# Turning keys, queries and normalised tokens in the DMA crossbar instead of on TensorE

## The chip, the cores and the metric

The kernel runs on one core of one Trainium2 chip. The metric is the device time of one execution in microseconds (us), the median of several runs. Engines: PE is TensorE's matmuls, PEld its weight loads, DVE is VectorE, ACT is ScalarE, POOL is GpSimd, SP is the sync engine. DMAs are issued from POOL (loads that cast from 32 to 16 bits) and from SP (stores, copies inside SBUF, the core's working memory, and the crossbar DMAs). The profile counts both kinds on the core's 16 DMA engines. L288 and the like are line numbers of the kernel; they differ from version to version.

## The reference, cut to what matters

Four batches of 768 tokens, 8 heads of 64. Attention goes by chunks of 32 queries, each with 8 memory keys and up to 56 keys around it. The result is the x of a feed-forward block: normalise x, multiply by a 512x2048 matrix, clip at zero, multiply by a 2048x512 matrix, add x.

```python
for c in range(nc):                       # chunks of 32 tokens
    k_full = concat([mem_k, k[:, :, l_start:r_end]])
    v_full = concat([mem_v, v[:, :, l_start:r_end]])
    scores = scale * q_c @ k_full.T
    out[c] = softmax(scores) @ v_full
x  = out.reshape(B, S, 512)
xn = (x - mean) / sqrt(var + 1e-6) * g_ln
out = x + maximum(xn @ w_ch1, 0) @ w_ch2
```

## The kernel before: the parts that the change touches

The matmuls here contract over partitions, so three things must be turned to have their features on partitions: keys (KT), queries (QZ) and the normalised tokens (xT). Before, all three were turned on TensorE by a matmul with the identity, and the result was copied out of PSUM, the memory into which the matmuls write.

```python
def turn_kq(pv, src, j, n):               # 128 of these matmuls a batch
    for r in range(8):
        for par in range(2):
            nc.tensor.matmul(
                out=pv[64 * par : 64 * par + 64, n * r : n * r + n],
                lhsT=src[0:n, 2 * j + par, r, :], rhs=identity[0:n, 0:n],
                is_transpose=True, start=True, stop=True,
                tile_position=(0, 64 * par))

def load_kq(b, which, lo=0, hi=96, h0=0, h1=H):   # runs of 512 values, 2 KB
    ...
        in_=dram(src, (b * H + h0) * HS + 512 * lo,
                 [[512, hi - lo], [HS, h1 - h0], [1, 512]]))

def turn_x(u, i, t, kind="att"):          # 4 matmuls a tile of 128 tokens
    for dt in range(4):
        nc.tensor.matmul(out=pv[:, 128 * dt : 128 * dt + 128],
            lhsT=xn[t % 3][:, 128 * dt : 128 * dt + 128], rhs=identity,
            is_transpose=True, start=True, stop=True)
    nc.scalar.copy(out=xT[u % 2][:, :, 128 * i : 128 * i + 128], in_=...)
```

The work is laid out by hand: eight units of three tiles of 128 tokens. A unit has 28 steps, 16 "up" steps (first matrix) and 12 "down" steps (second matrix). The attention of the following unit, the turns and the loads are hung on these steps. Units 2 and 4 prepare batches 2 and 3.

```python
elif u in (2, 4):
    attend(((1, 8, 8, 12), (4, 8, 10, 14), (11, 17, 17, 21)))   # scores, values, norm, turn_x
    b = u // 2 + 1
    for j, step in ((0, 17), (2, 23)):
        at(step, kq_block, b, j, 0, NG, "mm")
        at(step, keep_rest)
    for h in range(H):
        at(2 + 2 * h, load_v_head, b, h)
    ...
elif following:
    attend(((12, 17, 17, 21), (14, 17, 17, 22), (18, 23, 23, 26)))
```

The softmax here doesn't subtract the row's maximum and nothing guards it: scores larger than these inputs give would overflow.

## Time and profile before

| | before |
|---|---|
| median time | 231.82 us (231.43 to 232.01, three runs); 231.62 with a fourth |
| span of the profiled run | 230.2 us |
| PE busy | 222.8 us, 97% |
| idle time of PE, by its list of waits | 3.7 us, all before 49 us |
| DVE, ACT, POOL busy | 54%, 52%, 30% |

Busy time is what the profile counts for an engine; the list of waits names, for each idle stretch, who ended it.

### The profile page before, as it was taken

The page shows a single profiled execution, that of the slowest core. Times are in us where ns is not written, and L with a number is a line of the kernel's source. Part 1 is how long each engine was busy: PE and PEld are TensorE (multiplying, and loading weights), DVE is VectorE, ACT ScalarE, POOL GpSimd, SP SyncE. Part 2 cuts the span into 40 slices and gives each one's busy share as a digit, 9 for nine tenths or more (in the row PEclk, how much of TensorE's full clock was granted, in tenths as well). Part 3 has the DMA queues.
Part 4 walks back from the last instruction along what each step waited for, and adds up shares of the span by engine and source line. Part 5 has one row for each costly group of instructions (what it writes and reads, how often), then busy time and mean ns, then how long its engine had stood idle before and what let it go on. Part 6 is the DMA issues. An engine that isn't in the chain of part 4 may idle for free.

```text
span 230.2 us, 5499 instructions
## 1 busy us (share of the span) xinstructions
PE 222.8 (97%) x2289; PEld 138.2 (60%) x2289; DVE 125.4 (54%) x290; ACT 119.0 (52%) x228; POOL 68.6 (30%) x125
## 2 busy tenths in 40 slices
PE   7989999899999999999999999999999999999993
PEld 2455776447765577555765577556765566557553
DVE  5746881475747639575336648674436542663222
ACT  3565648253894576655355367654356335534200
POOL 6973343877360380530001370410001200030000
PEclk9999999999999999999999999999999999999999
DMA  5999999999999999548921199543001200111012
GB/s 80 169 90 203 201 211 150 125 200 226 121 69 126 226 145 36 37 77 119 236 48 48 48 127 23 37 99 106 0 3 46 90 4 0 47 48 46 0 48 93
DMA packets 50307, 21.91 MB, mean 95 GB/s; under 512 B 37817, under 2 KB 46777, under 8 KB 50234
## 3 DMA queue, kind: packets, MB, share of 16 engines
q0 software_dynamic: 45680, 14.23, 90.1%
q1 hardware_dynamic: 4602, 7.33, 10.5%
q8 instruction: 18, 0.29, 0.6%
q14 instruction: 7, 0.06, 0.1%
HBM read 28.48 MB, written 6.29 MB: 151 GB/s over the span
## 4 chain that ended last, share of the span: by engine, by line
PE 77%; DMA 16%; POOL 2%; DVE 2%; issue 1%; POOLq 0%
PE mm L319 32%; PE mm L336 32%; DMA w2c<-in_moe_w_ch_dram 13%; PE att L238 4%; DMA V<-in_v_dram 3%; PE att L258 3%; PE att L176 3%; PE att L296 2%; POOL V L114 2%; PE mm L354 2%; PE mm L176 1%; DVE QZ L374 1%; DVE V L379 0%; DVE V L378 0%; DVE osb L359 0%
## 5 line engine op out<-in xcount | busy, mean ns | idle before, releaser
L319 PE MATMUL mm<-xT,w1c 128*128 128x384 f16 x512 | 88.3, 326 | 0.0
L336 PE MATMUL mm<-w2c,rT 128*128 128x512 f16 x368 | 87.4, 379 | 0.2 <-DMA w2c<-in_moe_w_ch_dram 0.2
L319 PEld LDWEIGHTS <-w1c 128*128 128x128 f16 x512 | 57.0, 114 | 24.2 <-issue 0.3
L327 DVE TENSOR_SCALAR rT<-mm 128x384 f16<-128x384 f32 x64 | 35.5, 556 | 35.3 <-PE mm L319 35.1
L336 PEld LDWEIGHTS <-rT 128*128 128x128 f16 x368 | 33.8, 98 | 34.0 <-issue 0.3
L325 ACT ACTIVATE rT<-mm 128x384 f16<-128x384 f32 x64 | 31.2, 489 | 35.9 <-PE mm L319 33.9
L245 ACT ACTIVATE AT<-att,band 96x512 f16<-96x512 f32 x48 | 30.1, 677 | 17.1 <-PE att L238 16.6
L287 POOL TENSOR_SCALAR veps<-squares 128x1 f32<-128x1 f32 x24 | 4.5, 188 | 109.9 <-ACT junk L284 95.1
L343 DVE SCALAR_TENSOR_TENSOR osb<-mm,rstd,xs 128x512 f32<-128x512 f32 x23 | 17.2, 749 | 30.9 <-PE mm L336 20.4
L114 POOL DMA_DIRECT2D V<-in_v_dram x24 | 21.5, 900 | 15.5 <-DMA V<-in_v_dram 4.5
L301 ACT COPY xT<-att 128x512 f16<-128x512 f16 x21 | 12.2, 581 | 23.8 <-PE att L296 23.8
L191 DVE COPY KT<-att 128x80 f16<-128x80 f16 (+3 forms) x44 | 18.4, 480 | 2.1 <-PE att L176 2.1
L278 DVE SCALAR_TENSOR_TENSOR xn<-xs,nmean,g_row 128x512 f16<-128x512 f32 x24 | 18.0, 752 | 0.9
L201 ACT COPY QZ<-mm 64x768 f16<-64x768 f16 (+1 forms) x18 | 13.6, 757 | 8.0 <-PE mm L176 7.8
L268 DVE RECIPROCAL rec<-att 128x8 f32<-128x8 f32 x24 | 4.9, 203 | 23.3 <-PE att L258 23.3
L284 ACT ACTIVATE junk<-xs,nmean 128x512 f16<-128x512 f32 x24 | 17.4, 724 | 0.1
L269 DVE SCALAR_TENSOR_TENSOR xs<-att,rec 128x512 f32<-128x512 f32 x24 | 16.6, 691 | 0.8
L238 PE MATMUL att<-QZ,KT 128*128 128x128 f16 x192 | 14.8, 219 | 0.9 <-ACT AT L245 0.6
L238 PEld LDWEIGHTS <-KT 128*128 128x128 f16 x192 | 12.6, 98 | 4.6 <-issue 1.4
L201 ACT COPY QZ<-att 64x384 f16<-64x384 f16 (+1 forms) x20 | 12.0, 598 | 5.3 <-PE att L176 5.1
L291 POOL TENSOR_TENSOR rstd<-veps,mhalf 128x1 f32<-128x1 f32 x24 | 13.3, 553 | 2.0
L258 PEld LDWEIGHTS <-AT 96*64 96x64 f16 x384 | 7.9, 111 | 8.7 <-issue 6.0
(63 smaller groups left out, 145.5 us busy)
## 6 DMA issues: line engine op xcount, KB each, us to landing
out_dram<-osb SPq DMA_DIRECT2D x23, 256.0 KB, 5.9
w1c<-in_moe_w_ch_dram POOLq DMA_DIRECT2D x4, 512.0 KB, 12.0
w2c<-in_moe_w_ch_dram POOLq DMA_DIRECT2D x4, 512.0 KB, 15.7
V<-in_v_dram POOLq DMA_DIRECT2D x20, 88.0 KB, 14.1
k<-in_k_dram POOLq DMA_DIRECT2D x2, 768.0 KB, 12.4
q<-in_q_dram POOLq DMA_DIRECT2D x2, 768.0 KB, 16.1
V<-in_v_dram POOLq DMA_DIRECT2D x16, 96.0 KB, 5.9
k<-in_k_dram POOLq DMA_DIRECT2D x3, 256.0 KB, 6.3
```

The costliest lines, as they stand in the source:

```text
L114: nc.gpsimd.dma_start(out=V[b % 2][r : r + hi - lo, g, :, 0:64], in_=dram(v, b * H * HS + lo * D, [[64, hi - lo], [HS, H], [1, 64]]),)
L191: copy(out=free(KT[b % 2], j * KC + 24 + 32 * ga + 8 * lo, [[KR, gb - ga], [8, m], [1, 8]]), in_=free(pv, lo, [[8, gb - ga], [1, m], [n, 8]]),
L201: copy(out=free(QZ[b % 2][rows, j, g0, par, :], 0, [[128, g1 - g0], [8, 8], [1, 8]]), in_=free(pv[rows, :], 8 * g0, [[8, g1 - g0], [1, 8], ...
L238: nc.tensor.matmul(out=p[:, gg, 128 * j : 128 * j + 128], lhsT=KT[b % 2][:, j, KR * g : KR * g + 128], rhs=QZ[b % 2][:, j, g, :, :], start ...
L245: nc.scalar.activation(out=free(a, 32 * c, [[512, 2], [64, 8], [1, 32]], KR), in_=free(p, 32 * c, [[512, 2], [64, 8], [1, 32]], KR), func= ...
L278: nc.vector.scalar_tensor_tensor(out=xn[i], in0=x, scalar=nmean[i], in1=g_row, op0=ALU.add, op1=ALU.mult,)
L284: nc.scalar.activation(out=junk, in_=xs[xi], func=ACTF.Square, bias=nmean[i], accum_out=squares[i],)
L319: nc.tensor.matmul(out=p, lhsT=free(w, i, [[4, 128]]), rhs=xT[u % 2][:, dt, 0 : 128 * n], start=(dt == 0), stop=(dt == 3),)
L325: nc.scalar.activation(out=o, in_=p, func=ACTF.Relu)
L327: nc.vector.tensor_scalar(out=o, in0=p, scalar1=0.0, scalar2=None, op0=ALU.max)
L336: nc.tensor.matmul(out=p, lhsT=rT[hc][:, 128 * i : 128 * i + 128], rhs=w2c[hc // 4][:, hc % 4, :], start=(hc == 0), stop=(hc == 15),)
L343: nc.vector.scalar_tensor_tensor(out=o, in0=p, scalar=rstd[t % 9], in1=xs[t % 9], op0=ALU.mult, op1=ALU.add,)
```

## The change

Its intent: take the turns off the bound engine. Keys and queries of batches 2 and 3 are loaded with one token per partition (runs of 64 values, 256 B) and turned by crossbar DMAs ("crossings" below), four a batch. The queries carry columns of zeros, so that the crossing writes the block layout that the scores want. x is turned by crossbar for two of the three tiles of unit 2 and for all later units. The key columns are laid out anew (memory keys last), and the schedule is moved. The core of the diff:

```diff
+    def load_k_tokens(b, t):
+        nc.gpsimd.dma_start(out=free(kraw[0], 512 * t, [[64, H], [1, 64]]),
+            in_=dram(k, b * H * HS + 128 * t * D, [[D, 128], [HS, H], [1, 64]]))
+    def cross_k(b, half):
+        nc.sync.dma_start_transpose(
+            out=free(KT[b % 2], half * 24 * KR + 16, [[KR, 24], [1, 64]]),
+            in_=kraw[0][64 * half : 64 * half + 64, 0:3072])
+    def cross_q(b, half):
+        nc.sync.dma_start_transpose(
+            out=free(QZ[b % 2], half * 24 * 128, [[64, 48], [1, 64]]), in_=qraw[0][rows, :])
     def turn_x(u, i, t, kind="att"):
+        if kind == "dma":
+            nc.sync.dma_start_transpose(
+                out=xT[u % 2][:, :, 128 * i : 128 * i + 128], in_=xn[t % 3])
+            return
 ... (unit 1)
-            for which in range(2):
-                at(1, load_kq, 2, which)
-            attend(late)
+            at(1, clear_raw)
+            for t in range(6):
+                at(23, load_tokens, 2, t)
+            attend(((16, 19, 19, 19), (17, 19, 20, 20), (21, 23, 23, 26)), "att")
 ... (units 2 to 6)
-            attend(((12, 17, 17, 21), (14, 17, 17, 22), (18, 23, 23, 26)))
+            attend(((9, 14, 14, 14), (11, 14, 15, 15), (16, 20, 20, 20)))
+            if u in (2, 4):
+                for half in range(2):
+                    at(21, cross_k, b, half)
+                for half in range(2):
+                    at(22, cross_q, b, half)
+                at(24, mem_cols, b); at(24, k_around, b)
+                at(25, v_mem, b);    at(25, v_around, b)
             if u == 3:
-                for which in range(2):
-                    at(2 + which, load_kq, 3, which)
+                for t in range(6):
+                    at(21, load_tokens, 3, t)
 ... (value rows and masks moved by 8 rows, place(), k_around(): cut)
```

More of the change, by code (lines that the diff above doesn't have):

```diff
@@ L34 @@
     KR = 96
-    KC = NG * KR + 32
     HD = 65
@@ L58 @@
     w2c = [sb.tile([128, 4, 512], FP16, name=f"w2c{i}") for i in range(4)]
-    k16 = [sb.tile([96, H, 8, 64], FP16, name=f"k16_{i}") for i in range(2)]
-    q16 = [sb.tile([96, H, 8, 64], FP16, name=f"q16_{i}") for i in range(2)]
+    kraw = [sb.tile([128, 4096], FP16, name=f"kraw{i}") for i in range(2)]
+    qraw = [sb.tile([128, 4096 if i else 6144], FP16, name=f"qraw{i}") for i in range(2)]
+    k16 = [t[0:96, 0:4096].rearrange("p (h r d) -> p h r d", h=H, r=8) for t in kraw]
+    q16 = [t[0:96, 0:4096].rearrange("p (h r d) -> p h r d", h=H, r=8) for t in qraw]
     V = [sb.tile([128, NG, H, HD], FP16, name=f"V{i}") for i in range(2)]
-    KT = [sb.tile([128, 4, KC], FP16, name=f"KT{i}") for i in range(2)]
-    QZ = [sb.tile([128, 4, NG, 2, 64], FP16, name=f"QZ{i}") for i in range(2)]
+    KT = [sb.tile([128, NG * 4 * KR + 32], FP16, name=f"KT{i}") for i in range(2)]
+    QZ = [sb.tile([128, NG, 4, 2, 64], FP16, name=f"QZ{i}") for i in range(2)]
     AT = [sb.tile([128, 2, H, 64], FP16, name=f"AT{i}") for i in range(3)]
@@ L112, in load_v_group @@
         lo, hi = max(64 * g - 16, 0), min(64 * g + 72, S)
-        r = 24 + lo - 64 * g
+        r = 16 + lo - 64 * g
         nc.gpsimd.dma_start(
@@ L120, in load_v_head @@
         nc.gpsimd.dma_start(
-            out=V[b % 2][24:88, :, h, 0:64],
+            out=V[b % 2][16:80, :, h, 0:64],
             in_=dram(v, (b * H + h) * HS, [[64, 64], [64 * 64, NG], [1, 64]]),
@@ L127, in v_around @@
         vt = V[b % 2]
-        nc.sync.dma_start(out=vt[8:24, 1:NG, :, :], in_=vt[72:88, 0 : NG - 1, :, :])
-        nc.sync.dma_start(out=vt[88:96, 0 : NG - 1, :, :], in_=vt[24:32, 1:NG, :, :])
+        nc.sync.dma_start(out=vt[0:16, 1:NG, :, :], in_=vt[64:80, 0 : NG - 1, :, :])
+        nc.sync.dma_start(out=vt[80:88, 0 : NG - 1, :, :], in_=vt[16:24, 1:NG, :, :])
     def v_mem(b):
@@ L133, in v_mem @@
         nc.sync.dma_start(
-            out=V[b % 2][0:8, :, :, :],
+            out=V[b % 2][88:96, :, :, :],
             in_=bass.AP(tensor=src.tensor, offset=src.offset,
@@ L166, in mem_cols @@
         nc.vector.tensor_copy(
-            out=free(KT[b % 2], 0, [[KC, 4], [KR, NG], [1, 8]]),
+            out=free(KT[b % 2], KR - 8, [[KR, 4], [4 * KR, NG], [1, 8]]),
             in_=bass.AP(tensor=src.tensor, offset=src.offset,
@@ L191, in keep_k @@
                 copy(
-                    out=free(KT[b % 2], j * KC + 24 + 32 * ga + 8 * lo,
-                             [[KR, gb - ga], [8, m], [1, 8]]),
+                    out=free(KT[b % 2], (4 * ga + j) * KR + 16 + 8 * (lo - 8 * ga),
+                             [[4 * KR, gb - ga], [8, m], [1, 8]]),
                     in_=free(pv, lo, [[8, gb - ga], [1, m], [n, 8]]),
@@ L201, in keep_q @@
         copy(
-            out=free(QZ[b % 2][rows, j, g0, par, :], 0, [[128, g1 - g0], [8, 8], [1, 8]]),
+            out=free(QZ[b % 2][rows, g0, j, par, :], 0, [[512, g1 - g0], [8, 8], [1, 8]]),
             in_=free(pv[rows, :], 8 * g0, [[8, g1 - g0], [1, 8], [n, 8]]),
@@ L230, in keep_rest, with place, clear_raw, load_q_tokens @@
         kept_later.pop(0)()
+    def place(b, g):
+        return g if b < 2 else g % 2 * (NG // 2) + g // 2
+    def clear_raw():
+        nc.gpsimd.memset(free(qraw[0], 64, [[256, 24], [1, 128]]), 0.0)
+    def load_k_tokens(b, t):
+        nc.gpsimd.dma_start(
+            out=free(kraw[0], 512 * t, [[64, H], [1, 64]]),
+            in_=dram(k, b * H * HS + 128 * t * D, [[D, 128], [HS, H], [1, 64]]),
+        )
+    def load_q_tokens(b, t, par):
+        nc.gpsimd.dma_start(
+            out=free(qraw[0], 1024 * t + 192 * par, [[256, H // 2], [1, 64]]),
+            in_=dram(q, (b * H + par) * HS + 128 * t * D, [[D, 128], [2 * HS, H // 2], [1, 64]]),
+        )
+    def load_tokens(b, t):
+        load_k_tokens(b, t)
+        for par in range(2):
+            load_q_tokens(b, t, par)
+    def cross_k(b, half):
+        nc.sync.dma_start_transpose(
+            out=free(KT[b % 2], half * 24 * KR + 16, [[KR, 24], [1, 64]]),
+            in_=kraw[0][64 * half : 64 * half + 64, 0:3072],
+        )
+    def cross_q(b, half):
+        rows = slice(64 * half, 64 * half + 64)
+        nc.sync.dma_start_transpose(
+            out=free(QZ[b % 2], half * 24 * 128, [[64, 48], [1, 64]]), in_=qraw[0][rows, :]
+        )
+    def k_around(b):
+        n, odd, kt = 24, 24 * KR, KT[b % 2]
+        for dst, src, m, w in (
+            (odd, 64, n, 16), (4 * KR, odd + 64, n - 4, 16),
+            (80, odd + 16, n, 8), (odd + 80, 4 * KR + 16, n - 4, 8),
+        ):
+            nc.gpsimd.tensor_copy(
+                out=free(kt, dst, [[KR, m], [1, w]]), in_=free(kt, src, [[KR, m], [1, w]])
+            )
     def scores(b, t):
@@ L235, in scores @@
         for gg in range(2):
-            g = 2 * t + gg
+            g = place(b, 2 * t + gg)
             for j in range(4):
@@ L239, in scores @@
                     out=p[:, gg, 128 * j : 128 * j + 128],
-                    lhsT=KT[b % 2][:, j, KR * g : KR * g + 128],
-                    rhs=QZ[b % 2][:, j, g, :, :],
+                    lhsT=KT[b % 2][:, (4 * g + j) * KR : (4 * g + j) * KR + 128],
+                    rhs=QZ[b % 2][:, g, j, :, :],
                     start=True, stop=True,
@@ L293, in turn_x @@
     def turn_x(u, i, t, kind="att"):
+        if kind == "dma":
+            nc.sync.dma_start_transpose(
+                out=xT[u % 2][:, :, 128 * i : 128 * i + 128], in_=xn[t % 3]
+            )
+            return
         pv = as16(slot("att")[:, 0, :]) if kind == "att" else as16(slot("mm")[:, :])
@@ L368, in clear_k @@
     def clear_k(i):
-        nc.vector.memset(KT[i][:, :, 8:24], 0.0)
-        nc.vector.memset(KT[i][:, :, NG * KR - 8 : KC], 0.0)
+        end = 4 * KR * (NG - 1)
+        nc.vector.memset(free(KT[i], 0, [[KR, 4], [1, 16]]), 0.0)
+        nc.vector.memset(free(KT[i], end + 80, [[KR, 4], [1, 8]]), 0.0)
+        nc.vector.memset(KT[i][:, end + 4 * KR : end + 4 * KR + 32], 0.0)
     def clear_q(i, par):
@@ L406 @@
             load_kq(0, which, 0, CUT, h, h + 4)
-    keep(counts[:, 0:1], counts[:, 0:1], 24, 0.0)
-    keep(counts[:, 1:2], counts[:, 1:2], -88, 0.0)
+    keep(counts[:, 0:1], counts[:, 0:1], 16, 0.0)
+    keep(counts[:, 1:2], counts[:, 1:2], -80, 0.0)
     make_identity(nc, identity)
@@ L427 @@
     nc.gpsimd.memset(zero2[:, 1:2], -NEG)
-    keep(band[:, 0:1], zero2[:, 0:1], -64, NEG)
-    keep(band[:, 1:2], zero2[:, 0:1], 40, NEG)
-    keep(zero2[:, 1:2], zero2[:, 1:2], -8, 0.0)
-    nc.gpsimd.tensor_tensor(out=band[:, 1:2], in0=band[:, 1:2], in1=zero2[:, 1:2], op=ALU.add)
+    keep(band[:, 0:1], zero2[:, 0:1], -56, NEG)
+    keep(band[:, 1:2], zero2[:, 0:1], 32, NEG)
+    keep(zero2[:, 1:2], zero2[:, 1:2], 88, 0.0)
+    nc.gpsimd.tensor_tensor(out=band[:, 0:1], in0=band[:, 0:1], in1=zero2[:, 1:2], op=ALU.add)
     for g in range(4, 6):
@@ L509, in at, with attend @@
             plan.setdefault(step, []).append((fn, args))
-        def attend(steps):
+        def attend(steps, kind="dma"):
             for i, (s0, s1, s2, s3) in enumerate(steps):
@@ L517, in attend @@
                 at(s2, norm, t % 6, t % 9)
-                at(s3, turn_x, u + 1, i, t % 6)
-                at(min(s3 + 1, 27), root, t % 6, t % 9)
-        late = ((16, 19, 19, 22), (17, 21, 21, 24), (19, 23, 23, 26))
+                at(s3, turn_x, u + 1, i, t % 6, kind if i == 2 or u == 0 else "dma")
+                at(min(s3 + 3, 27), root, t % 6, t % 9)
         if u == 0:
@@ L534 @@
                 at(15, load_v_group, 1, g)
-            attend(late)
+            attend(((16, 19, 19, 22), (17, 21, 21, 24), (19, 23, 23, 26)), "att")
             at(26, mem_cols, 1)
@@ L543 @@
                 at(0, load_v_group, 1, g)
-            for which in range(2):
-                at(1, load_kq, 2, which)
-            attend(late)
-        elif u in (2, 4):
-            attend(((1, 8, 8, 12), (4, 8, 10, 14), (11, 17, 17, 21)))
-            b = u // 2 + 1
-            for j, step in ((0, 17), (2, 23)):
-                at(step, kq_block, b, j, 0, NG, "mm")
-                at(step, keep_rest)
-            for h in range(H):
-                at(2 + 2 * h, load_v_head, b, h)
-            at(21, mem_cols, b)
-            at(21, v_mem, b)
-            at(22, v_around, b)
-        elif following:
-            attend(((12, 17, 17, 21), (14, 17, 17, 22), (18, 23, 23, 26)))
+            at(1, clear_raw)
+            for t in range(6):
+                at(23, load_tokens, 2, t)
+            attend(((16, 19, 19, 19), (17, 19, 20, 20), (21, 23, 23, 26)), "att")
+        elif following:
+            attend(((9, 14, 14, 14), (11, 14, 15, 15), (16, 20, 20, 20)))
+            if u in (2, 4):
+                b = u // 2 + 1
+                for h in range(H):
+                    at(2 + 2 * h, load_v_head, b, h)
+                for half in range(2):
+                    at(21, cross_k, b, half)
+                for half in range(2):
+                    at(22, cross_q, b, half)
+                at(24, mem_cols, b)
+                at(24, k_around, b)
+                at(25, v_mem, b)
+                at(25, v_around, b)
             if u == 3:
-                for which in range(2):
-                    at(2 + which, load_kq, 3, which)
+                for t in range(6):
+                    at(21, load_tokens, 3, t)
         for step in range(16 + 4 * n):
```

## The prediction

> **What bounds the kernel now.** I read the page from the top: busy shares first, then the slices, then the chain of waits.
>
> ```profile
> PE 222.8 (97%) x2289; PEld 138.2 (60%) x2289; DVE 125.4 (54%) x290; ACT 119.0 (52%) x228; POOL 68.6 (30%) x125
> ...
> PE   7989999899999999999999999999999999999993
> ...
> PEclk9999999999999999999999999999999999999999
> DMA  5999999999999999548921199543001200111012
> ```
>
> TensorE is busy for 97% and, after the first quarter, in every slice; its clock is always full; no other engine passes 54%. The DMA row is full up to slice 16 and mostly empty later: transfers have room from about 90 us on. A busy TensorE could still be waiting inside its pipeline, so I looked at who ends its idle time: the list of its waits sums to 3.7 us, the last of them at 48.9 us. The chain of work that ended last, in order of time, is on VectorE, GpSimd and DMA until 48.9 us (the last of it the load of w2c) and then on TensorE alone, matmul after matmul, until the last eviction at 226.7 us. So after 49 us a microsecond taken from TensorE is a microsecond of the kernel, unless a new wait appears. One unit of three token tiles looks like this in the chain (start, length, what):
>
> ```profile
> 79.44 1.30 PE mm L319 x8
> ...
> 90.00 0.35 PE att L296 x4
> ...
> 91.65 0.22 PE att L296 x4
> ...
> 94.63 0.68 PE att L176 x32
> 95.32 0.68 PE mm L176 x32
> ...
> 99.56 0.22 PE att L296 x4
> ...
> 101.50 0.80 PE att L176 x32
> 102.31 0.68 PE mm L176 x32
> 102.99 3.56 PE mm L336 x16
> 106.55 8.45 PE mm L319 x52
> ...
> 130.59 1.30 PE mm L319 x8
> ```
>
> L319 and L336 are the two products of the feed-forward part, which stay. L296 turns normalised tokens, L176 turns keys and queries. The unit with keys and queries to turn runs from 79.44 to 106.55 = 27.1 us, the next, without, from 106.55 to 130.59 = 24.0 us.
>
> **What the Trainium skill says.** (1) "VectorE: DVE Perf Modes", section "The three transpose paths": a 128x128 bf16 turn is 390 ns on TensorE and 1309 ns by the DMA crossbar. Here TensorE's turn is cheaper: one L296 matmul lasts 219 ns and four in a row cost the chain 0.22 us, because they overlap. So the crossbar is slower; it gains only by taking the work off the bound engine. (2) "DMA: Bandwidth & Descriptors", section "Latency and other measured facts": a DMA transpose was measured at 261 GB/s. The trace before has no such DMA, so no run shows it yet. (3) The same page, "Specifications": below 512 B a DMA does not reach line rate. The trace agrees: the value loads read 256 B runs (they land as 128 B), and in the one-microsecond windows of batch 3's six first loads (6 x 64 x 12 = 4608 runs) data flows from 133 to 139.8 us: 6.8 us x 16 engines / 4608 = 24 ns a run and engine, 62 to 135 GB/s; batch 2's took 81.9 to 89.8, 27 ns.
>
> **The change, part by part.**
>
> Removed from TensorE: per batch 2 and 3, 128 turns of keys and queries. In the chain above they are 0.68 + 0.68 + 0.80 + 0.68 = 2.84 us; batch 3's four pieces are the same, 0.68 + 0.68 + 0.80 + 0.68. Together 5.7 us. Check: the two kinds of unit differ by 27.1 - 24.0 = 3.1 us each. Also removed are 17 of the 24 turns of x (two of the three for unit 2, all for units 3 to 7): 17 x 0.22 = 3.7, and with the two pieces of 0.35 and 0.36 that hide a short wait 4.0 us. The order of the built program confirms both: 3929 rows on TensorE instead of 4577, 648 fewer = 2 x (256 + 68). Sum on the path: **9.7 us**.
>
> Removed elsewhere: the evictions of these turns: on VectorE two batches of KT copies (12 a batch, four each of 1064, 230 and 225 ns, 6.1 us a batch), on ScalarE QZ copies (16 of 0.79 us, 12.7 us) and 17 xT copies of 0.58 us (9.9 us). Both engines are at half load, so this is worth nothing directly; it only makes evictions of L319 less likely to queue.
>
> Added on DMA: keys and queries come token by partition. Before, a batch was 2 x 96 x 8 = 1536 runs of 2 KB; now it is 2 x 768 x 8 = 12288 runs of 256 B. At 24 to 27 ns, an estimate, that is 12288 / 16 x 24..27 = 18 to 21 us a batch, and the batch's values behind them (6144 runs) another 9 to 10 us. Then four crossbar DMAs: 2 x 64 x 3072 x 2 B + 2 x 64 x 6144 x 2 B = 2.36 MB a batch (half of the query bytes are the padding zeros). At the page's 261 GB/s that is an estimate of 9.0 us, plus landing.
>
> Added on GpSimd: one clear of 3072 columns, early, and four small copies inside KT per batch. The only small copies I can scale from are the 128x128 operations at 235 and 293 ns; 160 to 480 columns give roughly 0.5 us each, 2 us a batch. They follow the key crossings, while the longer query crossings are still running, so they should be hidden.
>
> Now the deadlines, with the chain shortened. Unit 1 ends near 78.9, unit 2 lasts 24.0 - 0.7 = 23.4 and ends near 102.3. Token loads are issued at unit 1's step 23, near 75 us, and land by 94 to 97. The crossings are placed at steps 21 and 22 of unit 2, six or seven down steps (0.87 us each) before its end: near 97. So the loads just make it. The scores of batch 2 now stand at step 9 of unit 3, ten up steps of 0.65 us after 102.3: 108.8. The crossings have 97 to 108.8 = 11.8 us for an estimate of 9.0 plus about 2 of landing, beside the value loads on the same engines (until 104 to 107). This is tight: I put an estimate of 2 us of wait on it. The values product follows at step 14, near 113; its data must land (107) and be copied around on the same in-order queue. Another 0.5 us. Batch 3 has its loads two steps earlier in the unit, and 1.5 us of wait seems enough.
>
> The turn of x by DMA: the last norm of a unit is at step 20, seven down steps before the next unit needs it. Values end 0.4 us after the step, the norm takes VectorE 1.9 us (0.20 + 0.69 + 0.08 + 0.15 + 0.75), so of 0.4 + 7 x 0.87 = 6.5 us about 4 remain for the DMA. One crossing of 128x512 should take 2 to 3 us. In units 2 and 4 it runs beside the loads and could be late by a microsecond. I allow 1 us in all for the five units.
>
> Sum: 231.8 - 9.7 + 3.5 + 0.5 + 1.0 = 227.1 if every allowance comes due. I choose **225.0**: the steps of the schedule were evidently moved for this (scores from 12 to 9, norms from 23 to 20), which speaks for waits that were seen and tuned out, so I count under half of the allowances.
>
> **Rivals.** (a) *Everything hidden*: the crossbar keeps up and TensorE never waits: 231.8 - 9.7 = 222.1 us. For it speaks the empty DMA row after 90 us; against it, the 12 us budgets that I find nearly used up. (b) *The crossing takes the place of the turns*: the sync queue handles DMAs in order, and if the crossings run at half the page's rate (18 us a batch instead of 9), scores of batches 2 and 3 each wait 6 to 8 us, the copying around of values is late behind it, and the time is 234 to 238. For it: small pieces are slow on this DMA, as the value loads show, and no run shows the crossbar. (c) *The loads are the bound*: eight times as many runs per batch. If a 256 B run costs 35 ns instead of 25, tokens land near 102 instead of 96, everything behind them slips by 6 us in batch 2 and less in batch 3: about 230. Against it: two windows give 24 and 27 ns. (d) *A late x*: if one crossing of 128x512 takes 6 us rather than 3, all five units lose 2 us and the gain is nil: 231 to 232.
>
> **Range and chances.** The floor is (a), with a little for denser matmuls: 220.5. The high end is a middling (b) or (d): 232.5. Centre 225.0. The border of faster by over 2% is 227.2: (a) and mild waits lie below it, 0.64. Within 2% (227.2 to 236.5) are (c), (d) and the milder half of (b), 0.29. Beyond, 0.07, if (b) and (c) join.
>
> **What would show it.** In the profile after: no L176 work after 65 us; TensorE's busy time near 213 us (222.8 - 9.7); units 3 to 6 near 23.4 us each; DMA slices full from about 75 to 107 us and again from about 120 to 150. Right or wrong is decided by TensorE's idle time before the first scores of batches 2 and 3 (releaser: the crossing, expected 0 to 3 us each), before the first values (0 to 1) and before each unit's first up matmul (0 to 1). A single one of these above 4 us makes the prediction wrong on the high side; if all are zero it is 222.

## The result, and the profile after

The changed kernel takes 254.0 us median (251.49 to 255.08, four runs) beside 231.62 us (230.75 to 232.01). It is slower by 9.6%: the ratio is 1.0957, 95% interval 1.0865 to 1.1048. Ratios here are the mean time of one kernel's fast runs over that of the other's of the same rounds, so not quite the ratio of the medians. It computes the right result.

The same lines of the page, after: busy time by engine, then the busy tenths in 40 slices of 6.3 us, TensorE's granted clock and the DMA share.

```profile
PE 221.9 (88%) x1965; PEld 131.8 (52%) x1965; DVE 116.2 (46%) x268; ACT 99.5 (40%) x195; POOL 100.4 (40%) x166
...
PE   8989999999999999466299899979158999999995
...
PEclk9999999999999999959769999999859999999999
DMA  5999999999949999999753999998981330131012
```

TensorE has two holes, in the 17th to 20th slice and in the 29th and 30th, and the clock falls in both. Its busy time hardly fell, 221.9 for 222.8 us, although 324 matmuls went, 9.7 us by the prediction's working: 5.1 us came back where matmuls ran at half the clock (below), 2.7 us lie before unit 1 starts (50.7 us busy for 48.1), and about 1 us is not placed. Who ended the idle time, from TensorE's list of waits (in all us, times, longest):

```profile
PE att L288 <- DMA QZ<-qraw: 14.8, 4, 5.0
PE mm L374 <- DMA xT<-xn: 8.4, 3, 5.9
...
PE att L308 <- DMA V<-V: 1.2, 1, 1.2
```

The scores (L288) wait for the query crossings, the first product of a unit (L374) waits for the crossing of x, once the values product waits for the copy around. In TensorE's timeline (start, length, what, idle before) the first hole is:

```profile
109.22 8.32 PE L374 MATMUL mm<-xT,w1c 128*128 128x384 f16 x40 [5.92 <-DMA xT<-xn]
119.47 0.38 PE L288 MATMUL att<-QZ,KT 128*128 128x128 f16 x4 [1.93 <-DMA QZ<-qraw]
124.88 0.59 PE L288 MATMUL att<-QZ,KT 128*128 128x128 f16 x4 [5.03 <-DMA QZ<-qraw]
```

40 matmuls of L374 take 8.32 us here and 6.66 us in the later units at full clock. And what the sync queue did in that time (its own timeline; the length is that of the issuing instructions, with the waits between them):

```profile
99.26 1.19 SPq L345 DMA_TRANSPOSE xT<-xn  x1
100.74 10.62 SPq L260 DMA_TRANSPOSE KT<-kraw  x2
111.65 10.72 SPq L267 DMA_TRANSPOSE QZ<-qraw  x2
```

The key crossings hold the queue for 10.6 us, the query crossings for 10.7 us. Two stretches of DMA activity while query crossings run (the columns are busy time of PE, PEld, DVE, ACT and POOL with counts, then clock, DMA share, GB/s):

```profile
113.00:117.00 4.00, 4.00 (x26) 2.82 (x25) 1.75 (x4) 1.47 (x3) 0.79 (x3) 1.00 1.03 150
119.00:124.00 5.00, 0.38 (x4) 0.26 (x4) 0.00 (x0) 0.00 (x0) 0.00 (x0) 0.89 0.86 141
```

Only the crossings move data there, at 141 to 150 GB/s, at a DMA share of 0.86 to 1.03.

The account of the profiled spans, 251.6 - 230.2 = 21.4 us: waits of TensorE for crossings and values +24.4 (14.8 + 8.4 + 1.2); the slow clock after waits +5.1 (8.32 for 6.66 us at 109 us; 2.77 for 1.46, 1.06 for 0.61 and 2.62 for 2.11 after 125 us; 2.58 for 1.46 after 185 us); the turns removed -9.7, by the prediction's working; unit 1 starts 1.2 us later in this run (53.07 for 51.89). Sum 21.0.

The drop of the clock is told in the Trainium skill, "TensorE: Matmul & The Clock Gate", section "Part 1: The HAM clock gate (the "warmup" mystery)": after an idle window of about 3.4 us TensorE falls to half clock. The half agrees: here it stopped at 103.3 us, and by microsecond windows the granted clock was 0.90 from 105 to 106 and 0.50 from 106 us on, until 112 us. The time agrees only roughly: the fall came about 2.5 us after this stop, 3.0 us after the one at 119.9 us and 4.3 us after the one at 176.6 us, while the waits of 1.9 us (to 119.5 us) and 1.7 us (to 170.0 us) left the clock at full.

### The profile page after: what moved, and what is told of

Its sections match the earlier page's. It is cut to its first block, busy times and chain, and to the rows that moved or that the text cites. A ratio compares the mean times of both kernels' runs of the same rounds, so it can differ in the third digit from the quotient of the medians.

```text
span 251.6 us, 4902 instructions
## 1 busy us (share of the span) xinstructions
PE 221.9 (88%) x1965; PEld 131.8 (52%) x1965; DVE 116.2 (46%) x268; ACT 99.5 (40%) x195; POOL 100.4 (40%) x166
## 3 DMA queue, kind: packets, MB, share of 16 engines
q1 hardware_dynamic: 32538, 14.28, 29.7%
## 4 chain that ended last, share of the span: by engine, by line
PE 70%; DMA 12%; SPq 11%; ACT 2%; DVE 2%; issue 1%; POOL 0%; ACTq 0%
PE mm L374 27%; PE mm L391 24%; SPq L267 6%; PE att L288 4%; SPq L260 4%; PE mm L365 3%; DMA QZ<-qraw 3%; PE att L308 3%; DMA V<-in_v_dram 3%; PE att L177 2%; DMA V<-V 2%; DMA KT<-kraw 2%; DMA xT<-xn 2%; PE mm L409 1%; PE att L365 1%; PE mm L177 1%
## 5 line engine op out<-in xcount | busy, mean ns | idle before, releaser
L374 PE MATMUL mm<-xT,w1c 128*128 128x384 f16 x512 | 92.5, 338 | 8.4 <-DMA xT<-xn 8.4
L391 PE MATMUL mm<-w2c,rT 128*128 128x512 f16 x368 | 84.7, 379 | 0.0
L374 PEld LDWEIGHTS <-w1c 128*128 128x128 f16 x512 | 57.7, 116 | 37.1 <-issue 14.1
L382 DVE TENSOR_SCALAR rT<-mm 128x384 f16<-128x384 f32 x64 | 35.5, 557 | 70.1 <-PE mm L374 70.0
L391 PEld LDWEIGHTS <-rT 128*128 128x128 f16 x368 | 34.6, 98 | 37.2
L288 PE MATMUL att<-QZ,KT 128*128 128x128 f16 x192 | 16.2, 228 | 15.7 <-DMA QZ<-qraw 14.8
L115 POOL DMA_DIRECT2D V<-in_v_dram x24 | 21.5, 899 | 12.0 <-DMA w1c<-in_moe_w_ch_dram 3.7
L288 PEld LDWEIGHTS <-KT 128*128 128x128 f16 x192 | 13.6, 102 | 20.7 <-issue 17.0
L249 POOL DMA_DIRECT2D qraw<-in_q_dram x24 | 18.8, 824 | 0.0
L121 POOL DMA_DIRECT2D V<-in_v_dram x16 | 12.0, 769 | 0.0
L243 POOL DMA_DIRECT2D kraw<-in_k_dram x12 | 11.6, 963 | 0.0
L365 PE MATMUL mm<-busy 128*128 128x512 f16 x32 | 10.4, 458 | 1.2 <-DVE counts L455 1.2
## 6 DMA issues: line engine op xcount, KB each, us to landing
w2c<-in_moe_w_ch_dram POOLq DMA_DIRECT2D x4, 512.0 KB, 15.3
```

Source lines behind the costliest of these rows:

```text
L115: nc.gpsimd.dma_start(out=V[b % 2][r : r + hi - lo, g, :, 0:64], in_=dram(v, b * H * HS + lo * D, [[64, hi - lo], [HS, H], [1, 64]]),)
L249: nc.gpsimd.dma_start(out=free(qraw[0], 1024 * t + 192 * par, [[256, H // 2], [1, 64]]), in_=dram(q, (b * H + par) * HS + 128 * t * D, [[D ...
L288: nc.tensor.matmul(out=p[:, gg, 128 * j : 128 * j + 128], lhsT=KT[b % 2][:, (4 * g + j) * KR : (4 * g + j) * KR + 128], rhs=QZ[b % 2][:, g ...
L365: nc.tensor.matmul(out=p, lhsT=busy[:, 0:128], rhs=busy, start=True, stop=True)
L374: nc.tensor.matmul(out=p, lhsT=free(w, i, [[4, 128]]), rhs=xT[u % 2][:, dt, 0 : 128 * n], start=(dt == 0), stop=(dt == 3),)
L382: nc.vector.tensor_scalar(out=o, in0=p, scalar1=0.0, scalar2=None, op0=ALU.max)
```

## The experiments

Three theories. **A**: the four crossings of a batch are slow by themselves (about 146 GB/s, 16 us instead of the 9 that the prediction allowed, in a place with 12). **B**: they are slow because the value loads of the same batch run beside them. **C**: turning x by crossbar is itself the loss. All runs are of the changed kernel with an edit; times of the kernel before in the same rounds stand beside each. The diffs are cut to the lines that matter; where turns or loads go back to TensorE, the steps that they hang on go back too.

**x_only: only x by crossbar.** Keys and queries go back to the loads and TensorE turns of the kernel before.

```diff
-                at(23, load_tokens, 2, t)           # and the same for batch 3
+                at(1, load_kq, 2, which)
-                    at(21, cross_k, b, half) ... at(22, cross_q, b, half) ... k_around
+                    at(step, kq_block, b, j, 0, NG, "mm"); at(step, keep_rest)   # steps 17, 23
```

> Keys and queries are loaded and turned as in the kernel before; only the 17 turns of x go through the crossbar, with the schedule of the changed kernel. Theory A (the crossings of keys and queries are slow by themselves: about 146 GB/s, 16 us a batch) and theory B (they are late because the value loads of the same batch share the engines) both expect the plain gain of the removed TensorE turns of x, 17 x 0.22 to 4.0 us: 227 to 229 us, no wait above 1 us for x. Theory C (x by DMA is itself the loss: its landing of 3 to 5 us is too long for the 4 us of room) expects 1 to 6 us of wait in each of units 3 to 7 and 233 us or more.

Measured: 234.56 us (232.16 to 235.97; before 231.55), ratio 1.008, interval 1.0005 to 1.0155. Neither expectation: the time is that of theory C, the place of the wait is not. The timeline of TensorE has one wait for x, in unit 2:

```profile
83.29 9.37 PE L374 MATMUL mm<-xT,w1c 128*128 128x384 f16 x40 [3.30 <-DMA xT<-xn]
```

3.3 us of wait and 9.37 for 6.66 us of work at low clock: 6.0 us lost at one place. Units 3 to 7 have none. In unit 1, where the crossing of this x is issued, the DMA engines were still busy with the keys and queries of batch 2 (issued at 65.9 and 66.7 us, landing 11.4 and 15.3 us later in the median) and with two stores of results. So theory C in its plain form falls, but this crossing, which met loads and stores, was late.

**kq_only: only keys and queries by crossbar.**

```diff
-                at(s3, turn_x, u + 1, i, t % 6, kind if i == 2 or u == 0 else "dma")
+                at(s3, turn_x, u + 1, i, t % 6, "att")
-            attend(((9, 14, 14, 14), (11, 14, 15, 15), (16, 20, 20, 20)))
+            attend(((9, 14, 14, 18), (11, 14, 15, 20), (16, 20, 20, 24)))
```

> Keys and queries by crossbar as in the changed kernel, all turns of x back on TensorE. Theory A and B: the waits of the scores for the query crossing stay (about 15 us in all, plus the slow clock after them), the wait for x of 8.4 us goes, 4.0 us of turns come back: 244 to 250 us. Theory C: most of the loss goes with x: below 238 us.

Measured: 248.27 us (before 231.55), ratio 1.073. No wait for x, 17.0 us of waits for the query crossings. The larger part of the loss is theirs.

**no_v: no value loads beside the crossings** (wrong result).

```diff
-                for h in range(H):
-                    at(2 + 2 * h, load_v_head, b, h)
```

> The changed kernel without the loads of values of batches 2 and 3 (wrong result on purpose; the copies around stay). Theory A: the query crossings still take 5.4 us each; x of unit 3 is in time (5.9 us less), the first key crossing takes 3 us instead of 7, but the scores of batch 2 still wait about 9 us and those of batch 3 about 6: 240 to 248 us. Theory B: the waits for the query crossing vanish too: below 234 us.

Measured: 247.06 us (before 231.55), ratio 1.068. The wait for x shrank to 0.6 us, the waits for the query crossings rose to 19.7 us. TensorE's wait, and the sync queue in batch 2:

```profile
PE att L288 <- DMA QZ<-qraw: 19.7, 4, 6.6
...
99.07 4.43 SPq L260 DMA_TRANSPOSE KT<-kraw  x2
103.78 11.36 SPq L267 DMA_TRANSPOSE QZ<-qraw  x2
```

Without any load beside them the four crossings hold the queue from 99.1 to 115.1 us: 16.1 us for 2.36 MB, 147 GB/s. Theory B falls as the explanation of the score waits. It holds for two smaller things: the key crossings of batch 2 held the queue for 4.4 us here and for 10.6 us beside the value loads, and x of unit 3 was late by 5.9 us only with them.

**half_q: half of each query crossing** (half of the queries are left from an earlier batch, wrong; the comparison with the reference still passed, because the scores are so small that the softmax hardly depends on them: the reference draws queries and keys at 0.1, which makes scores of about 0.01, an estimate. So a passed comparison says little about the turning of keys and queries in any run here).

```diff
-            out=free(QZ[b % 2], half * 24 * 128, [[64, 48], [1, 64]]), in_=qraw[0][rows, :]
+            out=free(QZ[b % 2], half * 24 * 128, [[64, 24], [1, 64]]), in_=qraw[0][rows, 0:3072]
```

> The changed kernel with only the first half of the columns of each query crossing (wrong result on purpose): 48 instead of 96 blocks of 64 rows by 64... in bytes 0.79 instead of 1.57 MB a batch. Theory A: each query crossing takes 2.7 us of the sync queue instead of 5.4, the scores wait some 5 us less per batch: 239 to 244 us. Theory B: the value loads still delay everything before the queries; with the same start the gain is under 3 us: 250 us or more.

Measured: 238.88 us (before 231.55), ratio 1.033, just below the range of theory A and far from that of B. With half the bytes the query crossings hold the queue for less than half the time:

```profile
PE att L288 <- DMA QZ<-qraw: 3.1, 3, 2.2
...
110.30 4.24 SPq L267 DMA_TRANSPOSE QZ<-qraw  x2
```

4.2 us instead of 10.7 for two, and the waits for them fell from 14.8 to 3.1 us. The count of packets says how a crossing is made up: the hardware queue had 32538 packets in the changed kernel and 26394 here, 6144 fewer for 1.57 MB, so 256 B a packet. A batch has 9216 such packets; 16.1 us x 16 engines / 9216 = 28 ns a packet and engine, about what a 256 B run of the loads costs (24 to 27 ns in the prediction). This is the pace of a whole batch, and not the least time that the engines need for such packets. The changed kernel has a stretch in which nothing but crossings moves, 1147 packets in one microsecond, which is 14 ns a packet and engine:

```profile
109.00:110.00 1.00, 0.78 (x3) 0.41 (x3) 0.00 (x0) 0.00 (x0) 0.00 (x0) 0.50 1.28 286
```

The first key crossing had just held the queue for 7.1 us beside the value loads, so packets had presumably piled up. The engines took them at 286 GB/s, twice the usual pace, and a DMA share near 1 is no sign that they are full (it is 1.28 here). So the usual 28 ns is more likely the pace of what feeds the engines; no run tests that by itself.

**x_late: x by crossbar only from unit 3 on.** As x_only, with the turns of unit 2 on TensorE and the steps of unit 1 as in the kernel before.

> As x_only, but the two turns of x for unit 2, which met the loads of keys and queries, are back on TensorE; x by crossbar only in units 3 to 7. If the loss of x_only was that one meeting (3.3 us of wait and about 2.7 us of slow clock after it): no wait for x and 15 turns less, 15 x 0.22 plus 0.3 = 3.6 us: 227.5 to 229 us. If x by crossbar costs in general: 231 us or more.

Measured: 228.17 us (226.63 to 229.41; before 231.31), ratio 0.984, interval 0.977 to 0.991. It is faster, though not clearly by 2%. No wait for x in the profile, and TensorE's busy time is 219.6 us for 222.8. So x by crossbar is worth about what its turns cost, where its crossings are in time.

**early: the same crossings, issued earlier.** This tests theory A from the other side: if the crossings only need more time than they got, earlier loads give it.

```diff
-                at(23, load_tokens, 2, t)
+                at(1, load_tokens, 2, t)
-                    at(21, load_tokens, 3, t)
+                    at(3, load_tokens, 3, t)
-                    at(21, cross_k, b, half) ... at(22, cross_q, b, half)
+                    at(6, cross_k, b, half)
+                at(15 if b == 2 else 8, cross_q, b, 0)
+                at(21, cross_q, b, 1)
+  (and x of unit 2 on TensorE)
```

> The changed kernel with the same loads and crossings, only issued earlier (token loads of batch 2 at step 1 of unit 1 instead of 23, of batch 3 at step 3 of unit 3 instead of 21; key crossings at step 6, query crossings at steps 15 or 8 and 21), x for unit 2 on TensorE. Theory A (a crossing of 2.36 MB takes 16 us at 146 GB/s, and the changed kernel gave it 12): with about 20 us of room the waits mostly go, 2 to 4 us left in batch 2: 223 to 227 us. Theory B (256 B runs saturate the engines whenever they are issued, the total is too much): waits of 10 us and more stay: 235 us or more.

Measured: 233.58 us (232.59 to 235.39; before 231.31), ratio 1.009, interval 1.002 to 1.015. That is in neither range. Twenty of the 22 us of loss are gone, and TensorE waits for no query crossing any more. But it waits 6.9 us for x in unit 3, and the sync queue shows why:

```profile
96.86 8.87 SPq L267 DMA_TRANSPOSE QZ<-qraw  x1
...
106.46 1.22 SPq L345 DMA_TRANSPOSE xT<-xn  x1
```

The third tile of x could be issued only at 106.5 us, behind a query crossing that held the queue for 8.9 us beside the value loads.

**early_nopad: without the zeros.** Queries are crossed unpadded into a spare tile, 0.39 MB instead of 0.79 a crossing, and GpSimd spreads them over QZ, whose zeros stay from the start. The queries of a tile also come by one load instead of two, so the run changes more than the padding.

```diff
-            out=free(QZ[b % 2], half * 24 * 128, [[64, 48], [1, 64]]), in_=qraw[0][rows, :]
+            out=free(QT, half * 24 * 64, [[64, 24], [1, 64]]), in_=qraw[0][rows, 0:3072]
+    def spread_q(b, half, copy):
+        for par in range(2):
+            pr = slice(64 * par, 64 * par + 64)
+            copy(out=free(QZ[b % 2][pr, 6 * half, 0, par, :], 0, [[128, 24], [1, 64]]),
+                 in_=free(QT[pr, :], half * 24 * 64, [[64, 24], [1, 64]]))
```

> As early, and the queries are crossed without the padding zeros (4 crossings of 0.39 MB, 10.9 us a batch instead of 16.3) into a spare tile and spread by GpSimd, 4 copies a batch of 64 x 1536. Theory A: no wait above 1 us left: 222 to 225 us. Theory B: as for early, 233 us or more.

Measured: 228.65 us (226.27 to 229.86; before 231.31), ratio 0.988, interval 0.982 to 0.994. Waits for x of 2.5 us in the profiled run, none for queries. The time is above the expectation, and the runs spread over 3.6 us.

**early2 and early2b: what is behind the crossings on the queue.** Both put the query crossings straight behind the key crossings at step 8. early2 also moves the last norm of a unit from step 20 to 18.

```diff
-                at(15 if b == 2 else 8, cross_q, b, 0)
-                at(21 if b == 2 else 8, cross_q, b, 1)
+                at(8, cross_q, b, 0)
+                at(8, cross_q, b, 1)
-            attend(((9, 14, 14, 14), (11, 14, 15, 15), (16, 20, 20, 20)))
+            attend(((9, 14, 14, 14), (11, 14, 15, 15), (16, 18, 18, 18)))     # early2 alone
```

> early_nopad with both query crossings of a batch straight behind the key crossings (step 8), so that no turn of x stands behind one on the sync queue, and the last tile of each unit two steps earlier (values and norm at 18 instead of 20), which gives its crossing 1.7 us more. If the 2.5 us of waits left in early_nopad are the late x alone: none above 0.3 us, 222.5 to 226 us, 1 to 2 us below early_nopad. If x lands as late as the loads let it, whatever the order: no change.

> As early2, with the norms at step 20 as in the changed kernel: only the order of the crossings differs from early_nopad. The wait of 0.4 us in unit 3 should go, those of 1.2 and 0.9 us in units 4 and 5, which stand beside the loads, should stay: 0 to 1 us below early_nopad, 225 to 228.5 us.

Measured: early2 230.08 us (225.40 to 232.06), early2b 230.33 us (226.66 to 231.57), before 232.08. By fast runs the ratios are 0.984 and 0.983; but that leaves out a slower group which here is the kernel's own, and by medians they are 0.991 and 0.992. Neither median met its expectation, and the runs of early2 fall in two groups: it ran twice near 226 (counted fast) and four times at 229.6 to 232.1 (counted slow, being over 1.5% above the fastest); early2b ran at 226.7 and 229.1 us (fast) and four times at 230.1 to 231.6 us (slow). Their profiles differ mainly in one place, x of unit 3 (L382 is the first product of these versions): a wait of 2.0 us with the clock at full in a fast run of early2, and in a slow run of early2b this line:

```profile
107.61 8.56 PE L382 MATMUL mm<-xT,w1c 128*128 128x384 f16 x40 [6.12 <-DMA xT<-xn]
```

x of unit 3 stands behind four crossings that start when the token loads have landed and run beside the value loads. That chain fills its room, and when it is a few microseconds late the clock falls too. The two profiles are of different kernels, so the groups are explained here only as far as the next run bears it out.

**early3: nothing behind the crossings of batch 2.** As early2, with x of unit 3 turned on TensorE too.

```diff
-            attend(((9, 14, 14, 14), (11, 14, 15, 15), (16, 18, 18, 18)))
+            attend(((9, 14, 14, 18), (11, 14, 15, 20), (16, 18, 18, 22)), "att") if u == 2 else ...
```

> early2 with the three turns of x for unit 3 back on TensorE, so that no turn of x stands behind the crossings of batch 2 on the sync queue. If what makes early2 jump between 225.4 and 232.1 us is that one wait (2.0 us in the profiled run, 6.1 in that of early2b, and the slow clock after a wait above 3 us): no wait for x above 1 us, all runs near 224.5 to 226.5 us (0.7 us of turns back). If the jumps are from elsewhere in the crossings: the spread stays.

Measured: 224.98 us (223.64 to 226.50, six runs; before 232.08), ratio 0.971, interval 0.966 to 0.976. Every run lies within 3 us, so the two groups are gone. The longest waits in TensorE's list after the first microseconds are:

```profile
PE mm L382 <- DMA xT<-xn: 0.9, 2, 0.6
PE att L316 <- DMA V<-in_v_dram: 0.9, 1, 0.9
...
PE att L296 <- POOL QZ L274: 0.6, 1, 0.6
```

This version computes the right result and beats both kernels: 7 us below the kernel before, 29 below the changed one.

**x_late_again**: the comparison for early3, in its rounds.

> x_late once more, on the chip and in the rounds of early3, to compare the two: 227 to 229 us, above early3 by 1.5 to 3 us.

Measured: 227.69 us (226.78 to 229.60), ratio 0.984. So of the 2.9% of early3 a little more than half is had by the crossing of x alone, in the moved schedule, without crossing keys and queries.

## Why the prediction was wrong, point by point

- **What bounds the kernel, and the sum of the turns.** This held. TensorE was the bound, and the turns are worth what the chain said: x_late took 15 of the 17 turns of x away: TensorE's busy time fell by 3.2 us and the median by 3.1 to 4.4 us, where the working gives 3.6. early3 took away the keys and queries and 12 turns of x, 5.7 + 12 x 0.22 = 8.3 us: busy time fell by 7.9 us, the list of waits grew from 3.7 to 4.8 us, and the median is 7.1 us lower. Unit 6 of the changed kernel, which nothing disturbs, ran from 204.24 to 227.59 = 23.35 us for the 23.4 predicted.
- **"At the page's 261 GB/s that is an estimate of 9.0 us."** This is the step that failed first. no_v measured 16.1 us for the 2.36 MB with nothing beside, 147 GB/s, and the last crossing lands 2 to 3 us after its issue ends (8.1 us from the start of an issue that lasts 5.8 in the median). The place had 11.8 us. The mechanism (a tight place between step 21 and step 9) was the one named; the term was mis-sized by 7 us a batch.
- **"I put an estimate of 2 us of wait on it", 1.5 for batch 3.** Measured 1.9 + 5.0 and 4.4 + 3.5 us; a single wait above 4 us was the prediction's own sign of being wrong on the high side. The reason that I gave for counting under half of the allowances, that the schedule had evidently been tuned for this, was an argument about the author and not about the profile, and it was wrong.
- **"I allow 1 us in all" for a late x.** Measured 5.9 + 0.7 + 1.7 us. The prediction had the time of one crossing about right (landing 2.4 us after its issue at the least, 2.9 in the median), but not what stands beside it: the last three value loads, issued until 99.6 us, took 9.2 us to land in the median, and x of unit 3, issued at 99.3 us among them, let the first product go only at 109.2 us. no_v shows it: 0.6 us of wait without them.
- **The slow clock.** No term of the sum. After the three holes it cost another 1.7, 2.3 and 1.1 us, 5.1 us in all. With the late x it is why rival (b), which named the right mechanism and about the right crossing time (18 us), stopped at 234 to 238; its 12 to 16 us of score waits came to 14.8, and the other 13.5 us are x and the clock.
- **Loads (rival c).** They were faster than expected: data of batch 2's tokens flowed from about 77.5 to 93 us by microsecond windows, 15.5 us for 768 runs an engine, 20 ns each for the estimate of 24 to 27. Not the cause.
- **Extra work on GpSimd.** 0.50 us for the first copy of 384 columns and 1.0 us for the other three, 1.5 us a batch where 2 were estimated, and hidden. What the prediction left out is the issuing: GpSimd issued the 18 token loads of batch 2 one by one from 76.9 to 91.3 us (0.8 to 1.0 us each), and the value loads behind them went out only from 93.6 to 99.6 us, where six of the eight had gone out from 80.8 to 85.3 us before. This put them beside the crossings of x and of the keys.

## What to carry to other kernels

Moving work from the bound engine to DMA moves it under another clock: count its packets, not its bytes, by a rate taken from packets of the same size in your own trace (here 576 packets an engine at 24 to 27 ns would have given 14 to 16 us instead of 9). That this comes so near the 16.1 us measured is partly luck: crossing packets also ran at 14 ns, so the loads and the crossings need not share a limit. Then look at what stands behind the new transfers on an in-order queue, because a short urgent one waits for a long one ahead of it. A place that is tight by a few microseconds costs more than the wait when TensorE's clock falls with it, so give such transfers room first, and take padding out of them.

## What the Trainium skill lacked or had wrong

- "DMA: Bandwidth & Descriptors", section "Latency and other measured facts", gives 261 GB/s for a DMA transpose of another kernel, and 350 to 400 for the contiguous case; "Advanced Engine Details and Errata", section "X-Bar Transpose (TRN2)", says that it is as fast as a regular DMA. Here crossings from SBUF to SBUF of 64 rows by 3072 or 6144 columns ran mostly at 141 to 150 GB/s with nothing beside them, 16.1 us for 2.36 MB; only for a microsecond or two, as from 109 to 110 us, at 286 GB/s.
- "DMA: Bandwidth & Descriptors" names 256 B in passing for crossbar transposes, but no page says what such a packet (128 values; 6144 packets for 1.57 MB) costs: 28 ns an engine over a batch here, 14 ns in the fastest microsecond.
- "VectorE: DVE Perf Modes", section "The three transpose paths", has 1309 ns for a 128x128 crossing, without the time until it can be used: one of 128x512 held the sync queue for 1.19 us and landed 2.4 to 4.7 us after its start where the trace has the landing, and about 10 us after it beside loads.
- No page says outright that a large crossing holds the issuing queue for microseconds (4.9 to 5.9 us for 0.79 MB, up to 8.9 us beside loads), so that a small one issued behind it waits. "DMA: Bandwidth & Descriptors" has only a count of sequencer cycles by tiles, in a comparison with the next chip.
